# Wider moving operands with unused result columns, and the last output weights loaded last, in a two-branch attention decode kernel

## The chip, the cores and the metric

The kernel runs on one core of a Trainium2 chip. The metric is the device time of one execution in microseconds (us), the median of several runs. The profiler also gives a "span", from the first to the last instruction of one profiled execution; the span is about 1.7 us below the reported time (443.9 against 445.62, 446.1 against 447.8) in nearly every run listed here; run 2 is the exception, with 2.0 to 2.8 us.

## The reference, cut to what matters

Two attention decode steps, A and B, of the same sizes, with one query token, are joined in the output. A attends to all 8192 positions, B only to the last 2048.

```python
# per branch: B=4 sequences, D=512, Hq=32 query heads, Hkv=8, Sk=8192, Dh=128, bf16
q = (x @ wq).reshape(B, Sq, Hq, Dh).transpose(0, 2, 1, 3)
k = jnp.repeat(k_cache, rep, axis=1)          # rep = 4 query heads share a key head
v = jnp.repeat(v_cache, rep, axis=1)          # branch B: only the last W = 2048 rows of both
scores = jnp.einsum("bhqd,bhkd->bhqk", q, k) * (Dh ** -0.5)
o = jnp.einsum("bhqk,bhkd->bhqd", softmax(scores), v)
out = o.transpose(0, 2, 1, 3).reshape(B, Sq, Hq * Dh) @ wo
# ... result: concatenate([A, B], axis=-1)
```

The caches and weights that are read are 185 MB by the profile. The arithmetic is small: each key head meets only four query rows per sequence.

## The kernel before

The work is cut into 40 units. Units 0 to 7 belong to branch B (four key heads of one sequence), units 8 to 39 to branch A (one key head of one sequence, 2 MB of K and 2 MB of V). In each unit TensorE (PE) transposes K (32 transposes of 128x128 fp32 words, each holding two bf16), multiplies the transposed K with the queries (64 score products), and multiplies V with the softmax weights (64 value products). The K or V block is the stationary operand, so the moving operand is only 8 or 4 columns wide in branch A.

```python
# score products of unit u, block k (8 blocks)
for pi in range(4):
    t = k * 8 + 2 * pi
    for e in range(2):
        if P == 0:                                  # branch A: 8 moving columns
            rhs = RQc[:, u % Bn, e, :]
        else:                                       # branch B: 16
            rhs = RQB[:, b, un["gg"], t // J, e, :]
        ins = pe.matmul(out=stb[:, t * CPT:(t + 2) * CPT], lhsT=ktv[:, pi, :, e],
                        rhs=rhs, start=(e == 0), stop=(e == 1))

# value products of unit u, piece c (4 pieces); CPT = 4 in branch A, 8 in branch B
for i in range(TQ):
    t = c * TQ + i
    s, j = t // J, t % J
    ins = pe.matmul(out=otb[:, s * CPT:(s + 1) * CPT], lhsT=V_sb[:, vs, t, :],
                    rhs=pt_cols(u, t * CPT, CPT), start=(j == 0), stop=(j == J - 1))
```

K and V have four buffers each. SyncE issues the loads in the order below, each as soon as its buffer is free. V of the last unit, 39, comes in four pieces and is the last load. Its output weights ("wo", 0.5 MB for four heads) are loaded early, during unit 8, from ScalarE's queue.

```python
wo_at = {7: [1, 2], 8: [NG - 1]}        # during unit 8: the weights of the last group
# ... SyncE's order at the end: K37, V36, K38, K39, V37, V38, V39 (4 pieces), out, out
```

The end, after unit 39's score products, is:

```python
for c in range(NQ):
    pe_PV(L - 1, c)                     # value products of unit 38
add(dve_norm(L - 1))
for c in range(NQ):
    pe_PV(L, c)                         # unit 39; piece c waits for V piece c
add(dve_norm(L))
pe_OPJ(L // Bn)                         # last group: 2 halves x 4 heads, 256 columns each
# ... then two additions on VectorE and two stores
```

## Time and profile before

| | before |
|---|---|
| time, us (median of 3 runs, range) | 450.13 (449.95 to 450.6) |
| span of the profiled run, us | 447.8 |
| TensorE busy | 373.4 us, 83% |
| mean granted TensorE clock (1.00 is full speed; a mean over stretches at full and at half clock) | 0.797 |
| VectorE / ScalarE / GpSimd busy | 44% / 40% / 9% |
| bytes moved, mean rate over the span | 185 MB, 413 GB/s |

Three rows of the page of the kernel before, in 40 equal slices of the span: the granted TensorE clock in tenths, the busy share of the 16 DMA engines in tenths (9 is 90% or more), and what they moved.

```profile
PEclk9996569989886899866596689867875986788596
DMA  8999999999999999999999999999999999999991
GB/s 337 411 415 438 413 421 415 420 421 423 423 422 421 425 422 425 424 429 427 427 427 430 430 424 426 430 428 427 429 426 427 426 430 429 426 424 430 430 403 65
```

The DMA engines are full in all slices between the first and the last, at 411 to 438 GB/s (403 in the last but one). Nothing that TensorE does faster in the middle can shorten that stream. The clock row is as uneven as the DMA row is even.

Second, the costliest TensorE group and the value products, from the page's groups: line, engine, operation, tiles, shapes and count, then busy us and the mean ns of one, then idle time of the engine just before and what ended most of it.

```profile
L332 PE MATMUL ps<-identf,K_sb 128*128 128x128 f32 x1280 | 217.1, 329 | 32.9 <-DMA K_sb<-in_A_k_cache_dram 17.5
L397 PE MATMUL ps<-PT,V_sb 128*128 128x4 bf16 (+1 forms) x2560 | 76.2, 165 | 3.6 <-DMA V_sb<-in_A_v_cache_dram 1.8
```

The value products of branch A hardly ever wait for V (1.8 us in the whole kernel): when their turn comes, V has long landed. TensorE trails the loads except at its waits for K, 17.5 us in 13 waits; in the chain of waits they come about every 40 us, once in a group of four units, the last of them before unit 37 at 411.1 us.

The end in the table of windows. After the window's length come busy us and instruction counts of PE, PEld (TensorE's loads of the stationary operand), DVE, ACT and POOL, then the granted clock, the DMA share and GB/s.

```profile
400.00:411.00 11.00, 8.99 (x160) 8.82 (x160) 4.10 (x9) 4.40 (x5) 0.71 (x4) 0.73 1.00 425
411.00:425.00 14.00, 13.01 (x171) 10.45 (x172) 5.46 (x14) 4.40 (x5) 1.22 (x4) 0.56 1.00 427
425.00:436.00 11.00, 10.53 (x167) 9.99 (x168) 7.43 (x15) 7.35 (x9) 1.37 (x4) 0.94 0.99 412
436.00:440.00 4.00, 3.35 (x105) 3.24 (x102) 1.29 (x3) 1.37 (x2) 0.35 (x1) 1.00 0.55 218
440.00:448.00 8.00, 5.17 (x126) 4.10 (x126) 2.08 (x7) 0.42 (x1) 0.46 (x2) 0.50 0.01 3
```

From 411 to 425 us TensorE is busy for 13.01 of 14 us at a clock of 0.56, and from 440 us, with the loads over, it runs at half clock. In between, the clock is 0.94 and 1.00 with the same narrow operands.

Lines of the timeline of that end (start, duration, engine, line, operation, tiles, shapes, count, idle before; "..." stands for lines left out).

```profile
411.14 1.09 PE L332 MATMUL ps<-identf,K_sb 128*128 128x128 f32 x8 [0.79 <-DMA K_sb<-in_A_k_cache_dram]
...
413.35 1.97 PE L332 MATMUL ps<-identf,K_sb 128*128 128x128 f32 x8 [0.41 <-ACT KT_sb L341]
...
424.83 2.69 PE L332 MATMUL ps<-identf,K_sb 128*128 128x128 f32 x16
...
440.17 3.31 PE L397 MATMUL ps<-PT,V_sb 128*128 128x4 bf16 x118 [0.82 <-issue]
443.52 0.17 DVE L592 TENSOR_TENSOR OTg<-ps,RL 128x4 bf16<-128x4 f32 x1 [1.33 <-PE ps L397]
...
443.79 1.86 PE L474 MATMUL ps<-W,OTg 128*4 128x256 bf16 x8 [0.31 <-DVE OTg L592]
```

Eight transposes of unit 37 take 1.09 us at full clock and 1.97 us at half. Unit 38 starts at 424.8 us, 13.7 us after unit 37, although a unit's loads take only 9.8 us (4 MiB at 427 GB/s). The last output product takes 1.86 us at half clock.

### The profile page before, as it was taken

What the parts mean: (1) busy time and instruction counts of PE and PEld (TensorE: products, weight loads), DVE (VectorE), ACT (ScalarE), POOL (GpSimd) and SP (SyncE); (2) the same over time, 40 slices, a digit from 0 to 9 for tenths busy, and PEclk for the clock granted to TensorE, in tenths of its full rate; (3) what the DMA queues carried; (4) which work ended last, traced back from release to release, by engine and by line L of the source; (5) the groups of instructions that cost most, each with busy time, mean ns of one, the idle gap of its engine ahead of it and who ended that gap; (6) DMA issues with size and microseconds to landing.
All of it is one profiled execution on the core that took longest, in us unless ns stands there. A gap on an engine that the chain in (4) does not pass through costs nothing.

```text
span 447.8 us, 14767 instructions
## 1 busy us (share of the span) xinstructions
PE 373.4 (83%) x6783; PEld 339.4 (76%) x6783; DVE 195.9 (44%) x451; ACT 179.2 (40%) x202; POOL 40.1 (9%) x126
## 2 busy tenths in 40 slices
PE   0685199899676999988998998899889998988997
PEld 0685199768561898878898887879878987878896
DVE  0354055656440455434363444344443544344363
ACT  1163045435330464434264434334442543435261
POOL 1100000001100011000010001000110100010010
PEclk9996569989886899866596689867875986788596
DMA  8999999999999999999999999999999999999991
GB/s 337 411 415 438 413 421 415 420 421 423 423 422 421 425 422 425 424 429 427 427 427 430 430 424 426 430 428 427 429 426 427 426 430 429 426 424 430 430 403 65
DMA packets 17270, 185.01 MB, mean 413 GB/s; under 512 B 1860, under 2 KB 2392, under 8 KB 4824
## 3 DMA queue, kind: packets, MB, share of 16 engines
q1 hardware_dynamic: 15096, 178.27, 94.4%
q10 hardware_dynamic: 2080, 6.30, 3.5%
q8 instruction: 22, 0.36, 0.3%
q14 instruction: 8, 0.07, 0.0%
q0 software_dynamic: 64, 0.01, 0.0%
HBM read 184.56 MB, written 0.01 MB: 412 GB/s over the span
## 4 chain that ended last, share of the span: by engine, by line
DMA 54%; PE 35%; issue 4%; ACT 3%; DVE 2%; POOL 0%; ACTq 0%; POOLq 0%
DMA K_sb<-in_A_k_cache_dram 41%; PE ps L332 19%; DMA W<-in_A_wq_dram 7%; DMA W<-in_B_wo_dram 6%; PE ps L397 6%; PE ps L371 5%; PE ps L483 3%; ACT KT_sb L341 3%; PE ps L278 1%; DVE KT_sb L340 1%; DVE Dt L543 0%; DVE M L505 0%; ACT PT L554 0%; PE ps L474 0%; PE ps L438 0%
## 5 line engine op out<-in xcount | busy, mean ns | idle before, releaser
L341 ACT ACTIVATE KT_sb<-ps 128x1024 bf16<-128x1024 bf16 x160 | 163.0, 1023 | 244.9 <-PE ps L332 243.1
L332 PE MATMUL ps<-identf,K_sb 128*128 128x128 f32 x1280 | 217.1, 329 | 32.9 <-DMA K_sb<-in_A_k_cache_dram 17.5
L332 PEld LDWEIGHTS ps<-identf,K_sb 128*128 128x128 f32 x1280 | 179.0, 170 | 46.2 <-DMA K_sb<-in_A_k_cache_dram 18.6
L340 DVE COPY KT_sb<-ps 128x512 int32<-128x512 int32 x160 | 110.4, 690 | 138.9 <-PE ps L332 137.7
L397 PE MATMUL ps<-PT,V_sb 128*128 128x4 bf16 (+1 forms) x2560 | 76.2, 165 | 3.6 <-DMA V_sb<-in_A_v_cache_dram 1.8
L371 PEld LDWEIGHTS ps<-RQc,KT_sb 128*128 128x128 bf16 x2048 | 72.9, 100 | 4.5 <-ACT KT_sb L341 1.2
L371 PE MATMUL ps<-RQc,KT_sb 128*128 128x8 bf16 x2048 | 74.3, 167 | 0.9 <-ACT KT_sb L341 0.8
L397 PEld LDWEIGHTS ps<-PT,V_sb 128*128 128x128 bf16 x2560 | 70.8, 97 | 3.9 <-DMA V_sb<-in_A_v_cache_dram 2.0
L575 POOL PARTITION_ALL_REDUCE LB<-L x40 | 17.3, 432 | 155.2 <-DVE L L566 155.2
L514 POOL PARTITION_ALL_REDUCE MB<-M x32 | 11.9, 371 | 173.3 <-DVE M L505 173.3
L483 PE MATMUL ps<-W,OL 128*4 128x512 bf16 x60 | 22.5, 537 | 4.8 <-DMA W<-in_B_wo_dram 4.8
L592 DVE TENSOR_TENSOR OTg<-ps,RL 128x4 bf16<-128x4 f32 (+1 forms) x40 | 6.9, 173 | 40.2 <-PE ps L397 40.2
L505 DVE TENSOR_REDUCE M<-ps 128x4 f32<-128x256 f32 (+1 forms) x40 | 19.1, 477 | 10.8 <-PE ps L371 10.8
L566 DVE TENSOR_REDUCE L<-PT 128x4 f32<-128x256 bf16 (+1 forms) x40 | 21.9, 547 | 3.3 <-ACT PT L554 2.8
L371 PE MATMUL ps<-RQB,KT_sb 128*128 128x16 bf16 x512 | 18.6, 171 | 2.1 <-issue 1.2
L371 PEld LDWEIGHTS ps<-RQB,KT_sb 128*128 128x128 bf16 x512 | 17.9, 99 | 3.0 <-issue 1.5
L554 ACT ACTIVATE PT<-Dt 128x256 bf16<-128x256 f32 (+1 forms) x40 | 18.1, 452 | 4.0 <-DVE Dt L543 2.0
L483 PEld LDWEIGHTS ps<-W,OL 128*4 128x4 bf16 x60 | 5.6, 104 | 15.3 <-issue 8.7
L278 PE MATMUL ps<-xT,W 128*128 128x4 bf16 x256 | 7.4, 165 | 10.9 <-DMA W<-in_A_wq_dram 10.6
L278 PEld LDWEIGHTS ps<-xT,W 128*128 128x128 bf16 x256 | 7.0, 101 | 11.1 <-DMA W<-in_A_wq_dram 10.7
L543 DVE TENSOR_TENSOR Dt<-ps,MB 128x256 f32<-128x256 f32 x32 | 13.3, 415 | 0.5 <-POOL MB L514 0.5
L257 PE MATMUL ps<-ident,xo_sb 4*128 4x4 bf16 x8 | 0.6, 170 | 14.2 <-POOL identf L617 14.2
(49 smaller groups left out, 64.6 us busy)
## 6 DMA issues: line engine op xcount, KB each, us to landing
K_sb<-in_A_k_cache_dram SPq DMA_DIRECT2D x32, 2048.0 KB, 32.0
V_sb<-in_A_v_cache_dram SPq DMA_DIRECT2D x31, 2048.0 KB, 36.0
K_sb<-in_B_k_cache_dram SPq DMA_DIRECT2D x16, 1024.0 KB, 28.2
V_sb<-in_B_v_cache_dram SPq DMA_DIRECT2D x16, 1024.0 KB, 28.2
W<-in_B_wq_dram SPq DMA_DIRECT2D x1, 4096.0 KB, 12.9
W<-in_A_wq_dram SPq DMA_DIRECT2D x1, 4096.0 KB, 30.0
W<-in_A_wo_dram ACTq DMA_DIRECT2D x8, 512.0 KB, 10.5
W<-in_B_wo_dram SPq DMA_DIRECT2D x1, 2048.0 KB, 29.1
```

Source lines behind the costliest of these rows:

```text
L278: ins = pe.matmul(out=bk[:, hl * Bn:(hl + 1) * Bn], lhsT=W1wq[:, c, hq * DH:(hq + 1) * DH], rhs=xT[:, P, c, :], start=(c == 0), stop=(c == ...
L332: ins = pe.transpose(out=bkf[:, pi * 128:(pi + 1) * 128], in_=K_sbf[:, slot, t0:t0 + 2, :].rearrange("p t d -> p (t d)"), identity=identf[ ...
L340: return e.tensor_copy(out=KT_sb.bitcast(I32)[:, tj % NKT, :], in_=bkf.bitcast(I32)[:, :])
L341: return e.activation(out=KT_sb[:, tj % NKT, :], in_=bk[:, :], func=ACTF.Copy)
L371: ins = pe.matmul(out=stb[:, t * CPT:(t + 2) * CPT], lhsT=ktv[:, pi, :, e], rhs=rhs, start=(e == 0), stop=(e == 1))
L397: ins = pe.matmul(out=otb[:, s * CPT:(s + 1) * CPT], lhsT=V_sb[:, vs, t, :], rhs=pt_cols(u, t * CPT, CPT), start=(j == 0), stop=(j == J - 1))
L483: ins = pe.matmul(out=opb[0:Bn, 0:D], lhsT=OL[:, i // REP, i % REP, :], rhs=wo_view[:, wg + i // REP, i % REP, :], start=(P == 1 and first ...
L505: return dve.tensor_reduce(out=M1[:, 0:NC].rearrange("p (s h) -> p s h", h=CPT), in_=stb[:, 0:NT * CPT].rearrange("p (s j h) -> p s h j", ...
L543: return dve.tensor_tensor(out=Dt[:, 0:NT * CPT].rearrange("p (s j h) -> p s j h", s=S, h=CPT), in0=stb[:, 0:NT * CPT].rearrange("p (s j h ...
L554: return act.activation(out=PT[:, u % NPT, 0:NW], in_=Dt[:, 0:NW], func=ACTF.Exp, scale=scale)
L566: return dve.tensor_reduce(out=L1[:, 0:NC].rearrange("p (s h) -> p s h", h=CPT), in_=PT[:, u % NPT, 0:NT * CPT].rearrange("p (s j h) -> p ...
L575: return pool.partition_all_reduce(LB[:, 0:NC], L1[:, 0:NC], channels=128, reduce_op=ReduceOp.add)
```

## The change

The intent: give TensorE more columns to stream, so that its clock stays up, at no cost because a matmul of few columns takes as long as one of many; and move the weights that are needed last to the end of the load order, so that everything else comes earlier. The core of the diff:

```diff
+    NW = 64
+    NR = 4
-        PT = sb("PT", [128, NPT, NT * 2 * REP], BF16)
+        PT = sb("PT", [128, NPT, NT * 2 * REP + NW], BF16)
# score products, branch A: the 8 columns four times (later products overwrite the surplus)
-                            rhs = RQc[:, u % Bn, e, :]
+                            rhs = RQc[:, u % Bn, e:e + 1, :].broadcast_to([128, NR, 2 * CPT])
+                            dst = stb[:, t * CPT:(t + 2 * NR) * CPT].rearrange("p (a c) -> p a c", a=NR)
# value products: 64 columns, of which 4 (or 8) are used
-                    ins = pe.matmul(out=otb[:, s * CPT:(s + 1) * CPT], lhsT=V_sb[:, vs, t, :],
-                                    rhs=pt_cols(u, t * CPT, CPT), start=(j == 0), stop=(j == J - 1))
+                    ins = pe.matmul(out=otb[:, s * NW:(s + 1) * NW], lhsT=V_sb[:, vs, t, :],
+                                    rhs=pt_cols(u, t * CPT, NW), start=(j == 0), stop=(j == J - 1))
# start: all of PT is cleared, since the surplus columns are read
+            pool.memset(PT[:, :, :], 0.0)
# end: two matmuls of 512 columns with unused results between the last value pieces
         for c in range(NQ):
             pe_PV(L, c)
+            if c < NQ - 1:
+                pe_filler(2)
# last output weights: not during unit 8, but after V39, one load per head
-        wo_at = {7: [1, 2], 8: [NG - 1]}
+        wo_at = {7: [1, 2]}
+        for i in range(REP):
+            op("sp", dma(wl_view[:, wl_g, i, :], wl_src[:, i, :]), waits=[...], inc=("WL", i))
# ... and the last output product goes head by head (4 heads x 2 halves), head i waiting for ("WL", i)
```

Cut: the semaphores of the new loads, and the normalisation, which now reads 4 or 8 of each 64 columns.

## The prediction

> **What bounds the kernel now.** The stream of loads. In the table of windows the DMA share is 1.00 to 1.01 from 20 to 430 us, at 416 to 429 GB/s; 185 MB at 427 GB/s are 433 of the span's 447.8 us. The Trainium skill's "DMA: Bandwidth & Descriptors" (Specifications) gives a fabric ceiling of 435 GB/s; the trace agrees, so a faster engine wins nothing in the middle. TensorE (PE) is second: 83% busy, mean granted clock 0.797. Eight transposes take 1.07 us where the clock is full and 1.97 us where it is half (timeline). The queue is deep (median 32 us from issue to landing of a K load), so late slots don't starve it.
>
> **Only the end is TensorE's.** The chain of waits hangs on K loads until 411.1 us and from there runs through TensorE, with short ScalarE evictions. Window 420-430: PE busy 9.94 of 10 us at clock 0.68. The four last V pieces (issued 410.0 to 411.3, landing after 26.9 to 29.3 us) land at about 437 to 440.6. PE starts the last-but-one unit's value product only at 438.9, finishes the last at 443.5, spends 1.86 us on the eight output matmuls (256 columns each, clock 0.50); the final store follows. Last load to end: 7.2 us.
>
> **What the change does.**
> 1. Score products of the full-length half: 8 to 32 moving columns; value products: 4 or 8 to 64. Now 32 value matmuls take 0.85 us, about 27 ns each, at either clock. Estimate: 64 columns cost about the same at full clock, double at half. The Trainium skill's "TensorE: Matmul & The Clock Gate" (Part 1) says sustained array activity releases the clock. I expect that wide operands count as activity and narrow ones hardly do: mean clock 0.80 to about 0.95. A unit's PE work is then about 4.3+1.7+1.8 = 7.8 us, below its 9.8 us of loads. In the middle this buys nothing. At the end PE keeps up with the loads instead of trailing by about 3 us.
> 2. The last output weights (0.5 MB, 1.2 us at 427 GB/s) leave the middle and come last: late K and V land 1.2 us earlier, the last load at about 440.5 as before. The output product goes head by head; only its last head (0.4 us) follows the last load.
> 3. Added: two 512-column fillers after each of three value pieces (about 0.43 us a pair at full clock, in waits of 1.2 us): free if the clock is up, up to 2.5 us lost if not. A memset of PT on GpSimd, estimated 2.3 us (RQA's 512 columns took 0.52 us), delays the first projection by as much, hidden by the deep queue.
>
> **Sum.** The last weights land at about 440.5; last head and two adds (0.41 us each) about 1.4 us; store 1.7 us as now: span 443.6, 4.2 us less. Reported time 446.1, range 444.6 to 449.4. Chances: faster by over 2%: 0.03; within 2%: 0.94; slower: 0.03.
>
> **What would show it.** Mean clock over 0.9; still 425 to 430 GB/s in the middle; value matmuls up by under 10 ns each at full clock; first transposes at about 16.5 instead of 14.2 us; the chain of waits ends in W loads, last head, add, store; last load to end 3 to 4 us instead of 7.2.
>
> **What would make it wrong.** The clock doesn't rise: 64 columns at half clock add 1.7 us per unit and PE may become the bound (slower). The last weights' 1 KB rows run slowly on engines that finish unevenly (GB/s falls from 414 to 48 over 431 to 441 us): the end comes 1 us later. A change of the DMA rate itself moves everything by 1% per 4 GB/s.

## More of the kernel before

The output product is done once per group of four units: unit 37, for example, also carries the transposes and products of the finished group of units 32 to 35.

## The result, and the profile after

| | before | after |
|---|---|---|
| time, us (median, range) | 450.04 (448.51 to 450.6), 4 runs | 446.83 (446.18 to 447.8), 4 runs |
| ratio, 95% interval | | 0.9938 (0.9915 to 0.996) |
| span of the profiled run | 447.8 | 446.1 |
| TensorE busy | 373.4 us | 348.1 us |
| mean granted clock | 0.797 | 0.950 |

Every ratio here is the mean time of one kernel's fast runs over that of the other's of the same rounds, so it is not quite the ratio of the medians. The gain of 0.6% is outside the noise.

The same three rows of the page after the change:

```profile
PEclk9998579999988999999999999999889998999899
DMA  8999999999999999999999999999999999999993
GB/s 336 417 407 439 414 421 417 419 420 422 424 424 424 429 422 423 426 426 432 428 428 426 428 432 426 428 424 425 430 429 429 423 426 432 430 425 425 428 415 113
```

The clock is now nearly full almost everywhere, and the load stream is as it was. The same two groups:

```profile
L351 PE MATMUL ps<-identf,K_sb 128*128 128x128 f32 x1280 | 182.8, 290 | 36.9 <-DMA K_sb<-in_A_k_cache_dram 20.2
L417 PE MATMUL ps<-PT,V_sb 128*128 128x64 bf16 x2560 | 90.0, 195 | 19.7 <-DMA V_sb<-in_A_v_cache_dram 17.9
```

The transposes, which were not changed, lost 34 us of busy time; the wide value products cost 14 us more. TensorE is now busy for 78% of the span instead of 83%, so it is not more busy time that raised the clock. TensorE now waits 17.9 us for V, ten times as much as before: in the middle it keeps up with the loads, and the time it wins there turns into waiting. The windows of the end:

```profile
400.00:411.00 11.00, 8.42 (x166) 7.99 (x167) 4.10 (x9) 4.36 (x5) 0.94 (x3) 1.00 1.01 427
411.00:425.00 14.00, 12.32 (x193) 10.58 (x192) 7.04 (x17) 5.54 (x7) 0.94 (x3) 0.88 1.00 427
425.00:436.00 11.00, 10.60 (x219) 10.14 (x219) 6.44 (x14) 7.57 (x9) 1.37 (x4) 1.00 0.99 406
436.00:440.00 4.00, 3.37 (x106) 3.01 (x103) 1.69 (x6) 0.42 (x1) 0.80 (x2) 1.00 0.57 214
440.00:447.00 7.00, 3.40 (x61) 2.39 (x59) 0.91 (x3) 0.00 (x0) 0.00 (x0) 0.99 0.02 5
```

The clock is up in all five stretches, but from 411 to 425 us it is 0.88: it still dipped once, in unit 37. The timeline shows it, and the fillers (L324, out of ident and RQA):

```profile
410.31 1.09 PE L351 MATMUL ps<-identf,K_sb 128*128 128x128 f32 x8 [1.15 <-DMA K_sb<-in_A_k_cache_dram]
...
412.52 1.78 PE L351 MATMUL ps<-identf,K_sb 128*128 128x128 f32 x8 [0.46 <-ACT KT_sb L360]
...
422.72 2.10 PE L351 MATMUL ps<-identf,K_sb 128*128 128x128 f32 x16
...
437.45 2.22 PE L417 MATMUL ps<-PT,V_sb 128*128 128x64 bf16 x70 [0.63 <-issue]
...
439.51 0.60 PE L324 MATMUL ps<-RQA,ident 128*128 128x512 bf16 x2
...
439.94 0.63 PE L417 MATMUL ps<-PT,V_sb 128*128 128x64 bf16 x16
...
440.40 0.60 PE L324 MATMUL ps<-RQA,ident 128*128 128x512 bf16 x2
...
440.84 0.63 PE L417 MATMUL ps<-PT,V_sb 128*128 128x64 bf16 x16
...
441.30 0.59 PE L324 MATMUL ps<-RQA,ident 128*128 128x512 bf16 x2
...
441.74 0.63 PE L417 MATMUL ps<-PT,V_sb 128*128 128x64 bf16 x16
442.40 0.17 DVE L612 TENSOR_TENSOR OTg<-ps,RL 128x4 bf16<-128x4 f32 x1 [2.79 <-PE ps L417]
...
442.67 1.03 PE L493 MATMUL ps<-W,OTg 128*4 128x256 bf16 x8 [0.31 <-DVE OTg L612]
```

The output product takes 1.03 instead of 1.86 us. But between 437.45 and 442.4 us TensorE has no wait at all: the three rounds of fillers and value products follow each other every 0.89 us. The last V piece was issued at 410.1 us, and the longest landing time of the four was 29.6 us, so it is taken to have landed at about 439.7 us; its products began at 441.74. The fillers do not stand in a wait here. They are the chain.

### The profile page after: what moved, and what is told of

Its sections match the earlier page's. It is cut to its first block, busy times and chain, and to the rows that moved or that the text cites. A ratio compares the mean times of both kernels' runs of the same rounds, so it can differ in the third digit from the quotient of the medians.

```text
span 446.1 us, 14783 instructions
## 1 busy us (share of the span) xinstructions
PE 348.1 (78%) x6789; PEld 317.0 (71%) x6789; DVE 195.2 (44%) x451; ACT 179.0 (40%) x202; POOL 42.0 (9%) x127
## 4 chain that ended last, share of the span: by engine, by line
DMA 57%; PE 32%; issue 4%; ACT 3%; DVE 3%; POOL 1%; DVEq 0%; ACTq 0%; POOLq 0%
DMA K_sb<-in_A_k_cache_dram 44%; PE ps L351 15%; PE ps L417 7%; DMA W<-in_A_wq_dram 7%; DMA W<-in_B_wo_dram 6%; PE ps L392 5%; ACT KT_sb L360 3%; PE ps L502 2%; PE ps L283 1%; DVE KT_sb L359 1%; DVE M L524 1%; DVE Dt L562 1%; ACT PT L573 1%; POOL PT L630 0%; PE ps L458 0%
## 5 line engine op out<-in xcount | busy, mean ns | idle before, releaser
L351 PE MATMUL ps<-identf,K_sb 128*128 128x128 f32 x1280 | 182.8, 290 | 36.9 <-DMA K_sb<-in_A_k_cache_dram 20.2
L351 PEld LDWEIGHTS ps<-identf,K_sb 128*128 128x128 f32 x1280 | 146.5, 147 | 50.8 <-DMA K_sb<-in_A_k_cache_dram 21.8
L417 PE MATMUL ps<-PT,V_sb 128*128 128x64 bf16 x2560 | 90.0, 195 | 19.7 <-DMA V_sb<-in_A_v_cache_dram 17.9
L417 PEld LDWEIGHTS ps<-PT,V_sb 128*128 128x128 bf16 x2560 | 81.7, 99 | 21.9 <-DMA V_sb<-in_A_v_cache_dram 19.2
L392 PE MATMUL ps<-RQc,KT_sb 128*128 128x32 bf16 x2048 | 76.3, 177 | 1.1 <-ACT KT_sb L360 0.7
L392 PEld LDWEIGHTS ps<-RQc,KT_sb 128*128 128x128 bf16 x2048 | 71.9, 97 | 4.1 <-ACT KT_sb L360 0.9
L502 PE MATMUL ps<-W,OL 128*4 128x512 bf16 x60 | 15.7, 405 | 3.6 <-DMA W<-in_B_wo_dram 3.6
L262 PE MATMUL ps<-ident,xo_sb 4*128 4x4 bf16 x8 | 0.6, 170 | 15.4 <-POOL identf L639 15.4
L502 PEld LDWEIGHTS ps<-W,OL 128*4 128x4 bf16 x60 | 4.6, 88 | 10.6 <-DMA W<-in_B_wo_dram 3.7
```

Of the source, the lines that this page charges most:

```text
L351: ins = pe.transpose(out=bkf[:, pi * 128:(pi + 1) * 128], in_=K_sbf[:, slot, t0:t0 + 2, :].rearrange("p t d -> p (t d)"), identity=identf[ ...
L392: ins = pe.matmul(out=dst, lhsT=ktv[:, pi, :, e], rhs=rhs, start=(e == 0), stop=(e == 1))
L417: ins = pe.matmul(out=otb[:, s * NW:(s + 1) * NW], lhsT=V_sb[:, vs, t, :], rhs=pt_cols(u, t * CPT, NW), start=(j == 0), stop=(j == J - 1))
L502: ins = pe.matmul(out=opb[0:Bn, 0:D], lhsT=OL[:, i // REP, i % REP, :], rhs=wo_view[:, wg + i // REP, i % REP, :], start=(P == 1 and first ...
```

## The experiments

The theory after this reading had three parts. The wide operands hold the clock up, and what that is worth is decided in the last units. The load order brings the last K and V about 1.2 us earlier. The fillers take back some of it. The main rivals: the gain comes from the load order alone, or the fillers are free or even needed for the clock.

The middle columns say what each version has; "chip" tells which runs were on the same one and share the runs of the kernel before.

| run | wide | weights last | fillers | chip | time, us: median (range) | ratio to before (95%) | mean clock of the runs |
|---|---|---|---|---|---|---|---|
| 1 no fill | both | yes | 0 | a | 445.82 (445.59 to 445.97) | 0.9924 (0.9901 to 0.9947) | 0.954 |
| 2 four fillers | both | yes | 4 | a | 449.09 (447.15 to 449.39) | 0.9990 (0.9964 to 1.0017) | 0.956 |
| 3 wide only | both | no | 0 | a | 446.87 (446.74 to 447.19) | 0.9949 (0.9926 to 0.9972) | 0.953 |
| 4 load last only | none | yes | 0 | a | 447.60 (447.17 to 448.86) | 0.9966 (0.9941 to 0.9991) | 0.795 |
| 5 the change | both | yes | 2 | b | 446.16 (445.85 to 447.58) | 0.9932 (0.9911 to 0.9953) | 0.953 |
| 6 wide end only | last two units | yes | 0 | b | 447.36 (445.42 to 449.75) | 0.9955 (0.9926 to 0.9985) | 0.810 |
| 7 wide scores only | scores | yes | 0 | b | 446.79 (446.18 to 448.21) | 0.9944 (0.9923 to 0.9965) | 0.850 |
| 8 wide values only | values | yes | 0 | b | 446.02 (445.52 to 446.99) | 0.9922 (0.9902 to 0.9941) | 0.933 |
| 9 no fill again | both | yes | 0 | c | 445.78 (445.57 to 445.94) | 0.9916 (0.9903 to 0.9930) | 0.955 |
| 10 best try | both | yes | 0 | c | 445.71 (445.52 to 446.10) | 0.9915 (0.9901 to 0.9929) | 0.947 |
| 11 the change | both | yes | 2 | c | 446.04 (445.78 to 446.73) | 0.9925 (0.9910 to 0.9940) | 0.957 |
| 12 pads only | both | yes | 0 | c | 445.65 (445.56 to 446.07) | 0.9915 (0.9901 to 0.9929) | 0.950 |

All twelve gave correct results. The kernel before had medians of 449.38, 449.83 and 449.67 us on the three chips, with a mean clock of 0.79 on each.

### The two halves of the change: runs 1, 3 and 4

Run 1 is the changed kernel without fillers:

```diff
         for c in range(NQ):
             pe_PV(L, c)
-            if c < NQ - 1:
-                pe_filler(2)
```

> The changed kernel without its fillers. Theory (the fillers are on TensorE's chain: in the changed kernel three rounds of filler pair and 16 value matmuls follow each other without a gap, 0.89 us each, 0.43 us of it fillers): the last normalisation comes 1.2 to 1.3 us earlier (near 441.2 instead of 442.4 us), the clock after 436 us stays full because the wide products carry it, and the time falls by 0.8 to 1.3 us against the changed kernel, to about 445.7; what may limit it is the last weights, landing near 441.1 us. Rival (the fillers fill waits for V or keep the clock up): no gain, or the output products go back from 1.03 to 1.86 us and the time rises by up to 0.8 us.

Run 3 keeps the wide operands and takes the weights' load and the output product back to what they were:

```diff
# from run 1
-        wo_at = {7: [1, 2]}
+        wo_at = {7: [1, 2], 8: [NG - 1]}
-        for i in range(REP):
-            op("sp", dma(wl_view[:, wl_g, i, :], wl_src[:, i, :]), waits=[...], inc=("WL", i))
# ... output product by halves again, waiting for ("W1", 3)
```

> The kernel before with the wide operands alone (weights loaded early, old output product, no fillers). Theory (the clock carries most of the gain): mean clock near 0.95, last unit's score product done about 1.5 us earlier than before, output products about 1.0 instead of 1.86 us: 2 to 2.5 us less than before, about 447.8 us. Rival (the gain is the load order): clock up, time within 0.5 us of before.

Run 4 keeps the load order and takes the columns back:

```diff
# from run 1, in effect (the edit sets nr = 1 and w = CPT)
-    dst = stb[:, t * CPT:(t + 2 * NR) * CPT], rhs = RQc[...].broadcast_to([128, NR, 2 * CPT])
+    dst = stb[:, t * CPT:(t + 2) * CPT],      rhs = RQc[...].broadcast_to([128, 1, 2 * CPT])
-    out=otb[:, s * NW:(s + 1) * NW], rhs=pt_cols(u, t * CPT, NW)
+    out=otb[:, s * NW:s * NW + CPT], rhs=pt_cols(u, t * CPT, CPT)
```

> The kernel before with the last output weights loaded last, head by head, alone (narrow operands, no fillers). Theory (clock carries most): mean clock stays near 0.80, the value product still ends by TensorE's chain; K lands 1.2 us earlier, so 0.7 to 1.2 us less than before, about 449.1 us. Rival (the load order is the gain): 2.5 us less or more, about 447 us.

The three shared a chip and the 11 runs of the kernel before, whose mean was 449.23 us. Against it the means are 2.29 us less with the wide operands alone (446.94), 1.41 us less with the load order alone (447.82), and 3.43 us less with both (445.80). The two parts nearly add up (2.29 + 1.41 = 3.70). Run 4 gained more than the 0.7 to 1.2 us expected of it, run 3 (2 to 2.5 us) did not. Neither rival holds: the load order alone leaves the clock at 0.795 and wins less than half, and the clock alone wins the larger share but not all. The separate sizes are uncertain by about 1 us each (the intervals are 0.2 to 0.25% to each side, nearly all of it from the kernel before); that run 3 is the faster of the two, by 0.88 us, does not rest on the kernel before.

Where the clock's share comes from is visible in run 4's timeline. It has the earlier loads, but unit 37's transposes at half clock, unit 38 starting at 423.7 us, and the output product at 1.86 us. (Its profiled run is one of its slower ones, 448.38 us; the median is 447.60.)

```profile
412.26 1.97 PE L351 MATMUL ps<-identf,K_sb 128*128 128x128 f32 x8 [0.46 <-ACT KT_sb L360]
...
423.73 2.83 PE L351 MATMUL ps<-identf,K_sb 128*128 128x128 f32 x16
...
442.53 1.86 PE L495 MATMUL ps<-W,OTg 128*4 128x256 bf16 x8 [0.31 <-DVE OTg L614]
```

In run 1 unit 38 starts 2.7 us earlier, the value products of the last two pieces wait for V, and the output product is short:

```profile
421.05 2.10 PE L351 MATMUL ps<-identf,K_sb 128*128 128x128 f32 x16
...
438.29 0.52 PEld L417 LDWEIGHTS ps<-PT,V_sb 128*128 128x128 bf16 x16 [0.27 <-DMA V_sb<-in_A_v_cache_dram]
...
439.55 0.64 PE L417 MATMUL ps<-PT,V_sb 128*128 128x64 bf16 x16 [0.62 <-DMA V_sb<-in_A_v_cache_dram]
440.23 0.17 DVE L612 TENSOR_TENSOR OTg<-ps,RL 128x4 bf16<-128x4 f32 x1 [2.29 <-PE ps L417]
...
440.50 1.03 PE L493 MATMUL ps<-W,OTg 128*4 128x256 bf16 x8 [0.31 <-DVE OTg L612]
```

The chain of waits of run 1 (start, duration, what; "issue" is time in which the engine waited for nothing that the profile shows) ends accordingly in a load, that of the last V piece:

```profile
409.87 29.63 DMA V_sb<-in_A_v_cache_dram
439.50 0.05 issue
439.55 0.65 PE ps L417 x16
440.20 0.02 issue
440.23 0.18 DVE OTg L612
440.41 0.09 issue
440.50 0.94 PE ps L493 x7
```

This is the state that the change was after: the loads decide the end, and only 0.65 us of value products, one normalisation, 1.03 us of output product, two additions and the store follow them. The last head of the weights, issued at 424.7 us and landing after 16.1 us, at about 440.8 us, comes after V but is waited for by nobody: the output product runs without a gap.

### The fillers: runs 2, 5, 9 and 11

Run 2 is the changed kernel with `pe_filler(4)` in place of `pe_filler(2)`.

> The changed kernel with four fillers in each of the three places instead of two. Theory (on the chain): 3 x 0.43 = 1.3 us later, about 448.1 us. Rival (in waits of about 1.2 us): no change within 0.4 us.

> The changed kernel itself, for a comparison on the same chip as the next three. Theory (its fillers stand on the chain when the clock dipped in the last group's unit and mostly inside waits for V when it did not): two kinds of runs, near 446.2 and near 447.6 us, median about 446.8; the slower ones with the lower mean clock.

> The changed kernel without its fillers once more, on the same chip as the changed kernel itself (next but one). Theory (fillers cost about 0.2 us in runs at full clock at the end, over 1 us in runs where the clock dips in the last group's unit): median about 445.8 us with a spread under 0.6 us, 0.3 to 1 us below the changed kernel's median; the difference lies in the changed kernel's slower runs. Rival (fillers are free): no difference.

> The changed kernel on the same chip as the version without fillers: median about 446.3 us, runs from 445.9 to 447.7, the slower ones where eight transposes of the last group's unit take 1.8 to 2.0 instead of 1.1 us.

Run 2 is 3.27 us slower than run 1 on the same chip (449.09 against 445.82), and loses the whole gain over the kernel before; it is 1 us above my expectation. Its twelve fillers are 12 x 0.22 = 2.6 us of TensorE time. The spans of its six runs have a median of 446.6 us, those of run 1 of 444.1 us, so 2.5 us of the loss lie within the span. The remaining 0.8 us lie outside it: the reported time is 2.0 to 2.8 us above the span in run 2 and 1.7 to 1.8 us in run 1; why is not known. The profiled run, without a dip of the clock in unit 37, is one of the quicker ones; its span (445.8 us) is 1.9 us above that of run 1 (443.9 us). The direction is settled: fillers at this place are on the chain.

For two fillers, the same-chip pair is runs 9 and 11. In the profiled runs, both without a dip in unit 37 (eight transposes in 1.09 us in each), the output product starts at 440.44 without fillers and at 440.91 with them, 0.47 us later; the spans are 443.8 and 444.3. The wait lines of run 9 say why it is not more:

```profile
438.23 0.64 PE L417 MATMUL ps<-PT,V_sb 128*128 128x64 bf16 x16 [0.18 <-DMA V_sb<-in_A_v_cache_dram]
...
439.49 0.64 PE L417 MATMUL ps<-PT,V_sb 128*128 128x64 bf16 x16 [0.62 <-DMA V_sb<-in_A_v_cache_dram]
```

The last V pieces are waited for 0.18 + 0.62 = 0.80 us, and three filler pairs take 1.3 us. The medians of runs 9 and 11 differ by 0.26 us (0.3 to 1 was expected), the means by 0.40 us, and the intervals overlap: on one chip the cost of two fillers is barely resolved. Taken over all chips, 15 runs of the changed kernel lie between 445.78 and 447.80 us (mean 446.47), and 11 runs without fillers between 445.57 and 445.97 us (mean 445.78). So the fillers cost 0.4 to 0.7 us on average, and most of what they cost is in the slower runs.

Why the spread comes with the fillers is suggested by run 10 (below), which has no fillers and whose profile caught a dip of the clock in unit 37, like the first profile of the change:

```profile
412.24 1.97 PE L351 MATMUL ps<-identf,K_sb 128*128 128x128 f32 x8 [0.46 <-ACT KT_sb L360]
...
422.15 2.10 PE L351 MATMUL ps<-identf,K_sb 128*128 128x128 f32 x16
...
436.82 3.62 PE L417 MATMUL ps<-PT,V_sb 128*128 128x64 bf16 x118 [0.56 <-issue]
...
440.74 1.03 PE L493 MATMUL ps<-W,OTg 128*4 128x256 bf16 x8 [0.30 <-DVE OTg L612]
```

Unit 38 starts 1.2 us later than in run 9 (422.15 against 420.97), but the output product only 0.3 us later (440.74 against 440.44): the waits for V take up the delay. In the first profile of the change the dip was 0.6 us longer (422.72), and the output product came at 442.67, 1.9 us later than in run 10; the remaining 1.3 us fit three filler pairs at 0.43 us. Without fillers the end has about 0.8 to 0.9 us of slack, and the fillers use it up. These are two profiles; the other slower runs have none, so that all of them are slow for this reason is not shown. Nor is it shown what makes the clock dip in unit 37 in some runs.

Run 5 was expected at a median of 446.8 us, in two kinds of runs, and came at 446.16 us. That its slower runs would have the lower mean clock held for only part of them: of the six runs of run 5 the slowest (447.58 us) had the lowest clock (0.939), but among the 15 runs of the change 446.89 us stands beside 0.954. The mean over the whole kernel hides where a dip falls.

### How the clock follows the columns: runs 6, 7 and 8

Runs 7 and 8 take the width from one kind of product each; run 6 keeps it only where `u >= L - 1`, that is in units 38 and 39.

```diff
# run 6, from run 1; nr and w then stand for NR and NW in the two products
+    nr = NR if u >= L - 1 else 1          # scores
+    w = NW if u >= L - 1 else CPT         # values
# run 7: nr = NR, w = CPT in all units; run 8: nr = 1, w = NW in all units
```

> Last weights last, no fillers, wide operands in the last two units only (the 38 before them narrow). Theory (most of what the clock gives is won in the last full units before the end, where narrow operands leave TensorE behind the loads, plus the output product): mean clock near 0.79, the last two units start as late as in the run with the load order alone, only the output product goes from 1.86 to about 1.03 us: about 446.8 us, 0.8 below that run, 1 above the run without fillers. Rival (the clock before the last two units is worth nothing): as the run without fillers, about 445.8 us.

> Last weights last, no fillers, wide score products, narrow value products. Theory (the clock follows the moving columns streamed: per full-length unit 768 narrow, 2304 here, 4608 with wide value products only, 6144 with both): mean clock between, near 0.84, time near 447 us. Rival (any widening lifts it): 0.95 and about 445.8 us.

> Last weights last, no fillers, wide value products, narrow score products. Theory (columns streamed, 4608 per unit): mean clock near 0.91, time near 446.2 us. Rival (value products alone carry all of it): 0.95 and about 445.8 us.

The mean clock rises with the moving columns that one full-length unit streams, counted from the code (64 score products and 64 value products):

| version | score columns | value columns | sum per unit | mean clock |
|---|---|---|---|---|
| before | 64 x 8 | 64 x 4 | 768 | 0.79 |
| 7, wide scores | 64 x 32 | 64 x 4 | 2304 | 0.850 |
| 8, wide values | 64 x 8 | 64 x 64 | 4608 | 0.933 |
| 9, both | 64 x 32 | 64 x 64 | 6144 | 0.955 |

This is the order and nearly the size that was expected, and it rules out that any widening at all, or only that of the value products, gives the whole rise. It is a rule for the mean over the kernel, not for each moment: with narrow operands the clock is also full at times, as from 430 to 440 us in the kernel before. The time follows to a point: run 7 is 0.8 us slower than run 8 by the medians, and its profile has the clock back at 0.50 after 440 us, with the output product at 1.86 us. Run 8 (446.02 us) is not to be told from the version with both (445.78 and 445.82 us on other chips): the wide scores add clock, but no time that these runs resolve.

Run 6 is inconclusive. Its median fits the theory's direction (447.36, where 446.8 was expected and the rival said 445.8), but its six runs spread over 4.3 us, from below run 1's best to the time of the kernel before. In its profile unit 37 had one group of eight transposes at 1.97 us and one at 1.50, and the output product was at full clock (1.03 us) as expected. How much of the gain needs the wide operands before unit 38 is left open.

### The start, and a try at the best version: runs 12 and 10

Run 12 clears only the surplus columns of PT at the start; run 10 does this too, and stores the second half of the output from ScalarE's queue.

```diff
# run 12, from run 1
-            pool.memset(PT[:, :, :], 0.0)
+            pool.memset(PT[:, :, NT * 2 * REP:], 0.0)
# run 10, in addition
-        op("sp", dma(out[:, 0, H2:D], osb[0:Bn, 0, H2:D]), waits=[("ocp", 2)], inc=("out", 2))
+        op("act", dma(out[:, 0, H2:D], osb[0:Bn, 0, H2:D]), waits=[("ocp", 2)], inc=("out", 2))
```

> No fillers, and the start clears only the 64 pad columns of each PT slot instead of all of PT (the memset took 2.02 us and came with first transposes 1.2 us later than before the change). Theory (the deep queue of loads hides the start): first transposes back at about 14.3 us, time within 0.3 us of the version without fillers. Rival (the late start costs): 1.2 us less, about 444.6 us.

> A try at the best version: no fillers, only the pad columns of PT cleared at the start, the second half of the output stored from ScalarE's queue. The theory says that the start is hidden behind the loads and that the last store's issue follows its add anyway: within 0.3 us of the version without fillers, about 445.7 us.

The first matmul starts at 14.03 us in run 12, at 16.16 us in run 9, and at 14.19 us in the kernel before. These 2.1 us are worth nothing: 445.65 against 445.78 us. The loads were already queued, and TensorE caught up. Run 10 is at 445.71 us: the other queue wins nothing either. The best version is therefore the change without its fillers (runs 1, 9, 10 and 12 are one result, 445.65 to 445.82 us), which beats the kernel before by 0.8% and the change by 0.1 to 0.2%.

## Why the prediction was right or wrong

The predicted range, 444.6 to 449.4 us around 446.1 us, holds the measured 446.83 us, and later medians of 446.16 and 446.04 us. Point by point:

- **The loads bound the kernel, the middle has nothing to win: right.** The rate is unchanged (422 to 432 GB/s from slice 10 to 38 after the change, 421 to 430 before), while TensorE lost 25 us of busy time. The gain in the middle reappears as waiting for V, 17.9 instead of 1.8 us.
- **Wide operands count as activity: right.** 0.797 to 0.950, where 0.95 was predicted. The prediction drew on the Trainium skill's "TensorE: Matmul & The Clock Gate" (Part 1), that sustained activity of the array releases a clock that is halved when idle. The trace agrees: eight transposes take either about 1.09 or about 1.97 us. The graded experiment (0.79, 0.850, 0.933, 0.955) shows what the page does not: the width of the products counts. From 440.17 us, 118 products of 4 columns without a gap (28 ns each) ran at a clock of 0.50 in the kernel before.
- **64 columns cost about the same as 4 at full clock: right.** The same page (Back-to-back issue gap) gives N/2.4 + 2.5 ns for the gap of matmuls with N columns at full clock, by which 29 ns is an estimate for 64 columns; its table puts 1 to 64 columns at the floor of about 25 ns, and it warns that the weight loads between the products can make the spacing larger. In the chain of waits, 32 value products, each with its weight load, take 0.80 us (25 ns each) before at full clock, and 0.94 us (29 ns each) in run 3. That they take double at half clock was right too: 1.89 us (59 ns each) at 116.85 us in the chain of run 1.
- **The load order brings K and V 1.2 us earlier: right.** The transposes of unit 37, which wait for its K, start at 411.14 us before and at 411.51 us in run 3 (weights early), at 410.05 and 410.06 us in runs 4 and 1 (weights last). The last V pieces were issued from 408.8 instead of 410.0 us, and took 0.3 to 0.4 us longer to land, so that they came about 0.9 us earlier (run 1: from 408.5 us, 1.2 us earlier).
- **"At the end PE keeps up with the loads": only partly right.** The 7.8 us per unit are those of an ordinary unit. Unit 37 carries the output product of the finished group as well. Even at full clock it runs from 410.22 to 421.20 us in the profile of run 5, 11.0 us, against the 9.8 us of its loads; with a dip it was 12.4 us. So TensorE still enters unit 38 late; in the profiles without fillers and without a dip it has caught up by the last V pieces.
- **"Free if the clock is up": this step failed.** The prediction put the fillers into waits of 1.2 us. After unit 37's delay there was too little waiting left: 0.18 and 0.62 us in run 9, none in the first profile of the change. They cost 0.47 us in a profile without a dip and about 1.3 us in the one with a dip, and the four-filler run shows the same with a larger dose. The clock was up at the fillers in all of these.
- **"Only its last head (0.4 us) follows the last load": wrong, and of little weight.** The output product needs the last normalisation, which needs the last V. All eight matmuls (1.03 us at full clock, 1.86 us at half) come after it in every version; the weights are there in time. The prediction had the chain end in the loads of the weights; it ends in fillers and value products with the fillers, and in V's last piece without them, where no dip delays unit 38 (run 1).
- **The sum.** The span was predicted at 443.6 us. Profiled runs without a dip in unit 37 had 444.1 and 444.3 us (runs 5 and 11), the one with a dip 446.1 us. The prediction then added 2.5 us for the reported time, apparently because it set the profiled span of 447.8 us beside the median of other, slower runs; the offset measured since is 1.7 us. Two terms were thus mis-sized in opposite directions: the end of the chain by 0.5 to 2.5 us too short, the offset by 0.8 us too long. That 446.1 us came so close is in part luck; the span is the better test, and it was too short.
- **The start: right in what mattered.** The memset took 2.02 us (2.3 estimated), the first transposes came at 15.4 us in the first profile and at 16.2 us in run 9 (16.5 predicted), and run 12 shows that this costs nothing.

## What to carry to other kernels

When a kernel is bound by its loads, look for the gain of a faster engine only where the loads end: here about 25 us of TensorE time were worth about 2 us. A TensorE that issues narrow matmuls can be "83% busy" and still run much of the time at half clock, as this one did. Here wider moving operands cost 14 us of busy time in the value products and gave back 34 us in the transposes. Before filler work is put into a wait, measure that the wait is there in the slow runs too, and check whether useful wide work already holds the clock.

## What the Trainium skill lacked or had wrong

- "TensorE: Matmul & The Clock Gate" (Part 1) speaks of how busy the engine was, but does not say what of a matmul counts. Here 64 products of 8 and 64 of 4 columns per unit, at about 25 to 28 ns each, beside 32 transposes, left the mean clock at 0.79 with TensorE 83% busy by the profile; 2304, 4608 and 6144 columns per unit gave 0.850, 0.933 and 0.955. That narrow matmuls hold the clock up less, and by how much width helps, is missing.
- The same page (Part 4) says that the full clock "doesn't engage" for transposes in its transpose mode. If the transposes here (the kernel calls `pe.transpose`) are of that kind, that they did not hold the clock up fits the low clock of the kernel before. But they do run at the granted clock once other matmuls hold it up: eight fp32 transposes of 128x128 took 1.07 to 1.09 us at a clock of 1.00 and 1.97 us at half.
- "DMA: Bandwidth & Descriptors" (Where 436 GB/s comes from) says without a condition that for transfers from HBM to SBUF the HBM side, about 358 GB/s, binds. With one core this kernel read 421 to 430 GB/s from HBM over 300 us. The same page says, just above that section, that about 358 GB/s is what each core gets when both cores of an HBM domain stream, so the condition is missing in this one passage and not in the page.
- No place was found in that page on how long SyncE is held by an issue when many loads are under way (median 28.5 us from issue to landing for the last V pieces). The four 128 KB loads of the last weights, in rows of 1 KB, held it for 1.7 to 8.3 us each, the 512 KB pieces of V just before them for 0.33 to 0.43 us. Here it cost nothing, since nothing else was left to issue; the cause was not tested.
